# A fused attention and gMLP block on one core: the key load cut in two and the first maxima moved, idle matmuls moved, and h rows computed between the scores and the weighted sum

## The chip, the core and the metric

The kernel runs on one core of a Trainium2 chip. The core has five engines with their own instruction streams: PE (TensorE, matmuls; the profile lists its weight loads apart, as PEld), DVE (VectorE), ACT (ScalarE), POOL (GpSimd) and SP, which here only issues DMAs. Matmul results land in PSUM, of which there are eight banks of 128 x 512 float32; operands lie in SBUF. The metric is the device time of one execution in microseconds (us), the median of several runs.

## What is computed

The reference is a transformer block on 2048 rows of width 512, in float32: attention with 32 heads of width 16, then a gated MLP whose gate mixes the rows.

```python
def _A_ref(x, wqkv, wo):                     # H = 32, Dh = 16
    qkv = ((x @ wqkv).reshape(B, S, 3, H, Dh)).transpose(2, 0, 3, 1, 4)
    scores = jnp.einsum("bhqd,bhkd->bhqk", qkv[0], qkv[1]) * Dh ** -0.5
    o = jnp.einsum("bhqk,bhkd->bhqd", softmax(scores), qkv[2])
    return o.transpose(0, 2, 1, 3).reshape(B, S, D) @ wo
def _B_ref(x, w_in, w_sp, b_sp, w_out):      # S = 2048, D = 512, Fh = 688
    z = gelu(x @ w_in)
    z2 = _layernorm(z[..., Fh:])
    g = jnp.einsum("ts,bsf->btf", w_sp, z2) + b_sp[None, :, None]
    return jnp.einsum("bsf,fd->bsd", z[..., :Fh] * g, w_out)
h = x + _A_ref(_layernorm(x), wqkv, wo)
out = h + _B_ref(_layernorm(h), w_in, w_sp, b_sp, w_out)
```

## The kernel before the change

The program has four stages, one after the other on PE.

**Projections** (up to about 168 us). The rows of x are normalised, transposed and multiplied by wqkv. Each number is held as two rounded parts, so that each product takes three matmuls (`mm3`, lines 92 to 95: the lines L93, L94 and L95 of the profile). One projection of 512 columns is twelve matmuls. `take` (L386 to L390) copies its result out of PSUM: ACT writes the first part (L85), DVE the second (L90), SP stores both to q_scr or k_scr in DRAM (L389). q, k and v come back from there in other layouts: `load_k` (L160) loads the keys of a group of four heads in six DMAs (L164), `load_q` the queries (L193), `load_uv` sums and differences of keys (L172).

**Maxima.** The softmax needs a bound for each row before the scores are used. `max_pair` (L204) returns eight steps per block of rows: each a matmul of queries with keys into one PSUM bank (L222), followed by a DVE maximum over the bank (L227), or by ACT's absolute value (L232) and a DVE combination (L236). In the order of issue, the first six steps touch the key columns 0 to 1535 and the uv tile, the last two the columns 1536 to 2047. The last 24 projections (`for j in range(24)`, L547) are interleaved with the first 88 of these steps: `ahead(6)` issues six of them in the middle of a projection, in the projections that the condition on L555 names. The steps of `ahead` take six PSUM banks in turn, the last four of them four banks in another order (L454).

**Attention** (L708 to L774). A unit is one group of four heads, one block of 512 queries and one block of 128 keys. One pass of the loop handles two units and has this order on PE, with n the number of the first unit (n = 0, 2, ... 510):

```
score, score        # unit n: 2 x 2 matmuls (L663), each followed by an ACT exponential (L666)
step, step          # two maxima steps of a later group
weigh(previous)     # weighted sum of unit n-1: eight matmuls (L674) that read the exponentials
step, step
score, step, score, step   # unit n+1
step
weigh(unit n)
step
```

The maxima run 11 passes ahead, so they end with n = 488, and from n = 490 a third PSUM buffer for scores is opened in the banks that they leave (`ps_l`). In the first pass there is nothing to weigh, and eight matmuls with no use (stand-ins, L735) stand in the place of `weigh(previous)`; they write the bank of the weighted sum, which in the projections was a bank of projection results. After a block of queries `gather` (L677) copies the weighted sum out and SP stores it.

**Rows of h before the end of attention.** `load_o` (L589) loads a block of 128 rows of the attention output and of the reciprocal sums (L593, L596), POOL multiplies them (L600), `split_o` (L603) cuts the product into two parts, `make_h` (L608) multiplies it by wo: twelve matmuls in four `mm3`. Two such blocks are made within the attention loop (L758 to L772): three products after the second weighted sum of each of the eight passes n = 492 to 506. Their splits stand on DVE at n = 490, 498 and 506, the loads behind n = 480, 484, 496 and 504. A block's result is added to x on DVE (L617), its statistics taken (L620, L624, L104 to L120), and it is normalised (L771).

**The MLP** (from about 1414 us) begins with the transpose of the first block (L862), the product of the third block of h (L917), the transpose of the second block, and so on.

The order of the instructions of PE, ACT, DVE and SP is the order of the code, within each of two regions marked `tc.manual_schedule`: one for the projections (L457), one for attention (L710). Where the end of one region and the start of the next fall against each other on an engine, and the whole order of POOL, are left to a scheduler. Each engine works its queue in order; an instruction waits for the data and buffers that it needs.

Of the kernel before, what the change touches and what calls it, by code (L numbers as in the profile page):

```python
# [32 lines left out]
LEAD = 11  # L33
KM = 50
PB = 6
FIRST = 3
RG = 64
VW = DH + 1
FB = [min(i * P, FH - P) for i in range(6)]
# [6 lines left out]
def block_kernel(ctx: ExitStack, tc: tile.TileContext, x, wqkv, wo, w_in, w_sp4, b_sp, w_out, out):  # L46
# [45 lines left out]
    def mm3(ps, lh, ll, rh, rl, first, last):  # L92
        nc.tensor.matmul(ps, lh, rh, start=first, stop=False)  # L93
        nc.tensor.matmul(ps, lh, rl, start=False, stop=False)  # L94
        nc.tensor.matmul(ps, ll, rh, start=False, stop=last)  # L95
# [61 lines left out]
        return 8 * (hg // 2) + 4 * t + 2 * (hg % 2) + p  # L157


    def load_k(hg, pieces=range(6)):  # L160
        for j in pieces:
            j, t = divmod(j, 2)
            h0 = DH * head(hg, 0, t)
            nc.sync.dma_start(  # L164
                kst[hg % 2][RG * t + j:RG * t + KS:3, :, :].bitcast(F32),
                k_scr[(0, 0, 1)[j], h0:h0 + 2 * DH, :].rearrange("(p r) s -> r p s", r=DH))


    def load_uv(hg, pieces=range(3)):
# [95 lines left out]
    with ExitStack() as pre:  # L265
# [180 lines left out]
        def ahead(k):  # L446
            for _ in range(k):
                m = done[0] // 8
                if not todo and m < LEAD:
                    steps = max_pair(m)  # L450
                    todo.extend(steps[i] for i in (0, 1, 3, 2, 4, 6, 5, 7))
                if todo:

                    todo.pop(0)(done[0] % 6 if done[0] < 8 * LEAD - 4 else (3, 0, 1, 2)[done[0] % 4])  # L454
                    done[0] += 1

        with tc.manual_schedule(engines={E.PE, E.Activation, E.DVE, E.SP}):  # L457
            takes = []

            def proj(kind, *which):  # L460

                def between(d):
                    if d == 0 and rest:
                        rest.pop(0)()
                    if d == 1 and takes:
                        takes.pop(0)()

                takes.append(kind(*which, between))

# [24 lines left out]
            put = load_wqk(0)  # L494
            proj(proj_v, 1)
            normal(2, 3)
            turn_x(2, 3)
            for sb in range(8, 12):
                load_x(sb)
            put()  # L500
            for g in range(3):
                a, b = 4 * g, 4 * g + 4
                mv = moments(4)
                if g:
                    proj(proj_v, a)
                    turn_x(a + 2, a + 3)
                    if g == 1:
                        load_x(14)
                        load_x(15)
                    stats(mv, b, b + 1)  # L510
                    proj(proj_v, a + 1)
                    stats(mv, b + 2, b + 3)
                    proj(proj_v, a + 2)
                    normal = scales(mv)
                    normal(b, b + 1)
                    proj(proj_v, a + 3)
                else:
                    proj(proj_v, 2)
                    stats(mv, 4, 5)
                    proj(proj_v, 3)  # L520
                    stats(mv, 6, 7)
                if g == 1:
                    load_q(0)
                proj(proj_qk, 0, g, 1)
                if not g:
                    normal = scales(mv)
                    normal(b, b + 1)
                if g == 2:
                    put = load_wqk(1)
                proj(proj_qk, 0, g, 0)  # L530
                turn_x(b, b + 1)
                if not g:
                    load_x(12)
                    load_x(13)
                normal(b + 2, b + 3)
            proj(proj_v, 12)
            turn_x(14, 15)
            proj(proj_v, 13)
            load_uv(0)
            proj(proj_qk, 0, 3, 1)  # L540
            put()
            proj(proj_qk, 0, 3, 0)
            proj(proj_v, 14)
            load_k(0)
            proj(proj_v, 15)

            for j in range(24):  # L547
                b, n, i = 1 + j // 8, j // 2 % 4, 1 - j % 2

                def between(d):  # L550
                    if d == 0 and takes:
                        takes.pop(0)()
                        if rest:
                            rest.pop(0)()
                    if d == 1 and j >= FIRST and (j % 3 < 2 or j == 23):  # L555
                        ahead(6)
                    if d == 3 and turned:
                        max_rows()

                if j in (2, 10):  # L560
                    put = load_wqk(b + 1)
                if j in (5, 13):
                    put()
                if j == 4:
                    load_v(0)
                if j in (8, 12):
                    load_q(j // 4 - 1)
                if j == 16:
                    fixed(kst[0])
                takes.append(proj_qk(b, n, i, between))  # L570
            takes.pop(0)()
            ahead(8 * LEAD - done[0])
# [27 lines left out]
        nc.gpsimd.tensor_mul(o, o, rc)  # L600
        os_[sb] = o

    def split_o(sb, eh="act"):  # L603
        o = os_.pop(sb)
        o2s[sb] = [e2.tile([P, DB, P], F32R, name=f"o2{i}", bufs=1) for i in range(2)]
        split(o2s[sb][0], o2s[sb][1], o, eh)

    def make_h(sb, acc, steps=range(DB)):  # L608

        o2, h = o2s[sb], xrs[sb]  # L610
        for d in steps:
            mm3(acc, o2[0][:, d, :], o2[1][:, d, :], wo2[0][:, d, :], wo2[1][:, d, :],
                d == 0, d == DB - 1)
        if steps[-1] < DB - 1:
            return
        o2s.pop(sb)
        nc.vector.tensor_add(h, acc, h)  # L617
        nc.sync.dma_start(h_scr[sb * P:(sb + 1) * P, :], h)
        hst[sb] = e2.tile([P, 6], F32, name="st")
        nc.vector.bn_stats(hst[sb], h)  # L620
# [24 lines left out]
    with ExitStack() as at:  # L645
# [47 lines left out]
        def load_weights(i):  # L693
# [11 lines left out]
            nc.sync.dma_start(t, src[:, a, f])  # L705
            split(dst[0][:, a, f], dst[1][:, a, f], t, "pool", "pool")

        units = [(hg, qb, kb) for hg in range(HG) for qb in range(NQ) for kb in range(NB)]  # L708
        prev, turn, later = None, [2], []
        with tc.manual_schedule(engines={E.PE, E.Activation, E.DVE, E.SP}):  # L710
            for n in range(0, len(units), 2):
# [16 lines left out]
                pts = [score(hg, qb, kb, 0), score(hg, qb, kb, 1)]  # L728
                step(2)
                step(0)  # L730
                if prev is None:

                    pv[0] = ps_v.tile([P, 512], F32, name="pv")
                    for j in range(4):
                        nc.tensor.matmul(pv[0][32 * j:32 * j + 32, :], vst[0][:, :32],  # L735
                                         vst[0][:, :512], start=True, stop=True)
                else:
                    weigh(*prev)
                step(1)
                if kb == 0 and n:  # L740
# [3 lines left out]
                step(0)  # L744
                pts1.append(score(hg, qb, kb1, 1))
                step(1)
                step(2)
                weigh(hg, qb, kb, pts)
                if turned:
                    max_rows()  # L750
# [3 lines left out]
                    invert()  # L754
                if n % 32 == 16 and n < 6 * 32:
                    load_weights(n // 32)

                if n in (480, 484, 496, 504):  # L758
                    load_o(h_rows[(480, 484, 496, 504).index(n)])
                if 492 <= n < 508:  # L760
                    i, d = divmod((n - 492) // 2, DB)
                    sb = h_rows[i]
                    if not d:
                        acc = later[0].tile([P, 512], F32, name="h")
                    make_h(sb, acc, [d])
                if n in (490, 498, 506):
                    split_o(h_rows[(n - 490) // 8], None)
                if n in (498, 506):
                    mv, rs = scale_h(sb)
                    hns[sb] = e2.tile([P, D], F32, name="hn", bufs=3)  # L770
                    nc.vector.tensor_scalar(hns[sb], xrs.pop(sb), mv[:, 0:1], rs,  # L771
                                            op0=ALU.subtract, op1=ALU.mult)  # L772
            weigh(*prev)
            gather(*prev[:2], e2)  # L774
    attn.close()
# [496 lines left out]
```

## Time and profile before

| | |
|---|---|
| median of 3 runs | 1874.13 us (1872.52 to 1876.24) |
| the profiled execution | 1873.93 us |
| its span, first to last instruction | 1872.2 us |
| PE busy, share of the span | 99% |
| DVE, ACT, POOL busy | 82%, 70%, 12% |
| attention, first pass to first transpose of the MLP | 168.07 to 1414.34 us |

The profile gives a time and a duration for each instruction, from the start of the span. A row of a timeline has the start, the time, the engine, the line of the code, the operation, the tiles written and read, the number of instructions that were merged into the row, and in brackets how long the engine had been idle before and what released it. A row of the chain of waits has a start, a length and what the program's end hung on in that time. A row of a table by stretches has, after the stretch and its length, the busy time and the number of instructions for PE, PEld, DVE, ACT and POOL, then the granted clock of PE as a share of the full clock, the share of the DMA engines and GB/s. A busy PE can be a PE whose matmul waits, since matmul ends are modelled; so the starts of the matmuls are what to read.

### The profile page before, as it was taken

Reading aid. Unit: us, or ns where it says so; the run is one execution under the profiler, and the core shown is the slowest. Engines: PE = TensorE matmul, PEld = TensorE weight load, DVE = VectorE, ACT = ScalarE, POOL = GpSimd, SP = SyncE. Lnnn points to the kernel's source line nnn. Section 1 sums busy time; section 2 is a strip of 40 time slices with the busy share of each in tenths; the row PEclk is TensorE's granted clock in tenths of the full one; section 3 lists DMA queues with packets and bytes.
Section 4 is the critical chain, followed back from the end, with each engine's and each line's share of the span. In section 5 each row is a group of like instructions: output and inputs, shape, how many; then the busy total and the mean of one; then the engine's idle time right before and its main releaser. Section 6 shows DMA issues by size and latency. Waiting matters only on the chain.

```text
span 1872.2 us, 32341 instructions
## 1 busy us (share of the span) xinstructions
PE 1861.8 (99%) x11606; PEld 1064.2 (57%) x11606; DVE 1527.3 (82%) x3048; ACT 1318.7 (70%) x1696; POOL 222.3 (12%) x300
## 2 busy tenths in 40 slices
PE   9999999999999999999999999999999999999999
PEld 6875444444444444444444444444437999999998
DVE  6478999999999999999999999999936666867654
ACT  3224888888888888888888888888885444434221
POOL 2241000011010100000000000000010756001111
PEclk9999999999999999999999999999999999999999
DMA  6687111221120111022012011100024554768552
GB/s 191 175 223 180 41 24 29 48 54 28 39 56 16 52 40 25 18 47 39 13 38 41 16 38 39 25 13 16 24 58 122 164 161 165 226 189 272 192 190 87
DMA packets 148392, 159.82 MB, mean 85 GB/s; under 512 B 62984, under 2 KB 93208, under 8 KB 146696
## 3 DMA queue, kind: packets, MB, share of 16 engines
q1 hardware_dynamic: 143448, 146.35, 29.0%
q10 hardware_dynamic: 4752, 11.41, 1.6%
q8 instruction: 91, 1.49, 0.3%
q14 instruction: 69, 0.57, 0.1%
q0 software_dynamic: 32, 0.01, 0.0%
HBM read 101.16 MB, written 55.61 MB: 84 GB/s over the span
## 4 chain that ended last, share of the span: by engine, by line
PE 98%; DMA 1%; ACT 0%; SPq 0%; DVE 0%; issue 0%; DVEq 0%; ACTq 0%
PE pv L674 27%; PE m L222 26%; PE s L663 13%; PE acc L93 6%; PE acc L95 6%; PE acc L94 6%; PE g L95 4%; PE g L94 4%; PE g L93 4%; PE tp L1156 1%; DMA kst<-k_scr 1%; PE tp L862 0%; DMA wg<-in_wqkv 0%; PE tp L366 0%; DMA k_scr<-part 0%; PE tp L222 0%
## 5 line engine op out<-in xcount | busy, mean ns | idle before, releaser
L666 ACT ACTIVATE pt<-s 128x1024 f32<-128x1024 f32 x1024 | 994.3, 1030 | 148.9 <-PE s L663 146.1
L227 DVE TENSOR_REDUCE mx<-m 128x1 f32<-128x512 f32 x1508 | 956.2, 683 | 102.2 <-PE m L222 58.7
L222 PE MATMUL m<-kst,qst 48*128 48x512 f32 x1508 | 604.8, 447 | 0.6 <-DMA kst<-k_scr 0.5
L674 PE MATMUL pv<-pt,vst 128*32 128x512 f32 x4096 | 549.6, 605 | 0.3 <-DVE o L682 0.3
L663 PE MATMUL s<-qst,kst 50*128 50x512 f32 x2048 | 465.7, 429 | 0.0
L222 PEld LDWEIGHTS m<-kst,qst 48*128 48x128 f32 x1508 | 262.6, 184 | 317.4 <-DVE mx L227 222.1
L663 PEld LDWEIGHTS s<-qst,kst 50*128 50x128 f32 x2048 | 222.7, 185 | 50.5 <-ACT pt L666 29.4
L222 PE MATMUL m<-uvs,qst 48*128 48x512 f32 x497 | 247.0, 497 | 0.0
L222 PEld LDWEIGHTS m<-uvs,qst 48*128 48x128 f32 x497 | 90.9, 183 | 205.4 <-DVE mx L227 204.6
L674 PEld LDWEIGHTS pv<-pt,vst 128*32 128x32 f32 x4096 | 82.3, 108 | 160.2 <-issue 154.7
L236 DVE CUSTOM_DVE_ANT_0 ab<-m,ab 128x512 f32<-128x512 f32 x249 | 169.1, 679 | 0.0
L232 ACT ACTIVATE ab<-m 128x512 f32<-128x512 f32 x248 | 149.3, 602 | 5.3 <-PE m L222 5.3
L87 POOL CAST mparts<-nm 128x16 fp32r<-128x16 f32 x32 | 6.3, 198 | 877.5 <-DVE nm L242 877.5
L802 ACT ACTIVATE ws<-a 128x512 fp32r<-128x512 f32 x80 | 45.7, 621 | 53.6 <-PE g L95 27.1
L93 PE MATMUL acc<-wi,hT 128*128 128x344 f32 x256 | 83.1, 325 | 0.0
L95 PE MATMUL acc<-wi,hT 128*128 128x344 f32 x256 | 81.7, 319 | 0.0
L94 PE MATMUL acc<-wi,hT 128*128 128x344 f32 x256 | 81.7, 319 | 0.0
L878 ACT ACTIVATE z<-acc 128x344 f32<-128x344 f32 x64 | 29.2, 458 | 63.4 <-PE acc L95 63.2
L803 DVE TENSOR_TENSOR ws<-a,ws 128x512 fp32r<-128x512 f32 x80 | 56.5, 749 | 13.2 <-ACT ws L802 13.1
L93 PE MATMUL g<-b,ws 128*128 128x344 f32 x192 | 62.6, 326 | 0.0
L95 PE MATMUL g<-t,ws 128*128 128x344 f32 x192 | 61.3, 319 | 0.0
L94 PE MATMUL g<-t,ws 128*128 128x344 f32 x192 | 61.2, 319 | 0.0
(202 smaller groups left out, 2147.5 us busy)
## 6 DMA issues: line engine op xcount, KB each, us to landing
a<-in_w_sp SPq DMA_DIRECT2D x80, 256.0 KB
qst<-q_scr SPq DMA_DIRECT2D x192, 64.0 KB
kst<-k_scr SPq DMA_DIRECT2D x48, 256.0 KB
z_scr<-z ACTq DMA_DIRECT2D x32, 344.0 KB
k_scr<-part SPq DMA_DIRECT2D x16, 512.0 KB
q_scr<-part SPq DMA_DIRECT2D x16, 512.0 KB
z<-z_scr SPq DMA_DIRECT2D x14, 344.0 KB
b<-z_scr SPq DMA_DIRECT2D x24, 172.0 KB
```

What stands on the lines that cost most here:

```text
L93: nc.tensor.matmul(ps, lh, rh, start=first, stop=False)
L94: nc.tensor.matmul(ps, lh, rl, start=False, stop=False)
L95: nc.tensor.matmul(ps, ll, rh, start=False, stop=last)
L222: nc.tensor.matmul(acc, q[r, p, c], keys[r, p], start=True, stop=True)
L227: nc.vector.reduce_max(at(t, e if t else e - 1), acc, axis=AX.X)
L232: nc.scalar.activation(ab[0], acc, AF.Abs)
L236: nc.vector.tensor_tensor_reduce(ab[0], acc, ab[0], 0.5, LOW, ALU.add, ALU.max, at(0, 0))
L663: nc.tensor.matmul(s[:, t, :], k[r, p, kb * P:(kb + 1) * P], q[r, p, :], start=True, stop=True)
L666: nc.scalar.activation(t, s, AF.Exp, scale=DH ** -0.5)
L674: nc.tensor.matmul(pv[0][32 * j:32 * j + 32, :], vst[hg % 2][:, c:c + 32], pts[j % 2][:, j // 2, :], start=kb == 0, stop=kb == NB - 1)
L802: nc.scalar.activation(hi, src, AF.Copy)
L803: (nc.gpsimd if el == "pool" else nc.vector).tensor_sub(lo, src, hi.bitcast(F32))
```

## The change

Five things are done.

1. The maxima start two projections sooner: `FIRST` goes from 3 to 1, and the condition becomes `j % 3`, so the calls of `ahead(6)` stand in j = 1, 2, 4, 5, ... 20, and the last four steps in j = 22. The steps use the six banks in turn to the end.
2. The first key load is cut at column 1536. The first part is issued after the projection `proj_v(12)`, the second where the whole load was issued. Six DMAs become twelve.
3. The stand-ins move from the place of `weigh(previous)` to the place behind the fourth score and the sixth maxima step of the first pass.
4. The products of h move ahead of the second weighted sum of a pass, behind the scores: three in the passes n = 490 and 492, two in each of the nine passes 494 to 510. These are the same 24 products. The end of a block (addition, split of the next block, statistics, normalisation) follows its twelfth product.
5. The loads move to n = 476, 482, 492 and 504. The first block is split on POOL behind n = 482, the second on DVE as before, the third on POOL behind the last product of the second, in the pass n = 510.

```diff
-FIRST = 3
+FIRST = 1
-    def load_k(hg, pieces=range(6)):
+    def load_k(hg, pieces=range(6), c=slice(0, S)):
...
-                kst[hg % 2][RG * t + j:RG * t + KS:3, :, :].bitcast(F32),
-                k_scr[(0, 0, 1)[j], h0:h0 + 2 * DH, :].rearrange("(p r) s -> r p s", r=DH))
+                kst[hg % 2][RG * t + j:RG * t + KS:3, :, c].bitcast(F32),
+                k_scr[(0, 0, 1)[j], h0:h0 + 2 * DH, c].rearrange("(p r) s -> r p s", r=DH))
...
-                    todo.pop(0)(done[0] % 6 if done[0] < 8 * LEAD - 4 else (3, 0, 1, 2)[done[0] % 4])
+                    todo.pop(0)(done[0] % 6)
...
             proj(proj_v, 12)
+            load_k(0, c=slice(0, 3 * 512))
             turn_x(14, 15)
...
-            load_k(0)
+            load_k(0, c=slice(3 * 512, S))
...
-                    if d == 1 and j >= FIRST and (j % 3 < 2 or j == 23):
+                    if d == 1 and j >= FIRST and j % 3:
                         ahead(6)
...
+    def h_products(sb, acc):
+        o2 = o2s.pop(sb)
+        for i in range(3 * DB):
+            d, a, b = i // 3, (0, 1, 0)[i % 3], (0, 0, 1)[i % 3]
+            yield nc.tensor.matmul(acc, o2[b][:, d, :], wo2[a][:, d, :], start=i == 0, stop=i == 3 * DB - 1)
...
+        def more_h(k):
+            for _ in range(k):
+                if not pieces:
+                    sb = h_rows[len(hns)]
+                    acc = later[0].tile([P, 512], F32, name="h")
+                    pieces.extend([sb, acc, h_products(sb, acc)])
+                sb, acc, products = pieces
+                next(products)
+                made[0] += 1
+                if made[0] % (3 * DB):
+                    continue
+                pieces.clear()
+                add_h(sb, acc)
+                split_o(h_rows[len(hns) + 1], *("pool", "pool") if hns else [None])
+                mv, rs = scale_h(sb)
+                hns[sb] = e2.tile([P, D], F32, name="hn", bufs=3)
+                nc.vector.tensor_scalar(hns[sb], xrs.pop(sb), mv[:, 0:1], rs,
+                                        op0=ALU.subtract, op1=ALU.mult)
...
-                if prev is None:
-                    pv[0] = ps_v.tile([P, 512], F32, name="pv")
-                    for j in range(4):
-                        nc.tensor.matmul(pv[0][32 * j:32 * j + 32, :], vst[0][:, :32],
-                                         vst[0][:, :512], start=True, stop=True)
-                else:
+                if prev:
                     weigh(*prev)
...
                 pts1.append(score(hg, qb, kb1, 1))
                 step(1)
+                if prev is None:
+                    pv[0] = ps_v.tile([P, 512], F32, name="pv")
+                    for j in range(4):
+                        nc.tensor.matmul(pv[0][32 * j:32 * j + 32, :], vst[0][:, :32],
+                                         vst[0][:, :512], start=True, stop=True)
                 step(2)
+                if n >= 490:
+                    more_h(2 + (n < 494))
                 weigh(hg, qb, kb, pts)
...
-                if n in (480, 484, 496, 504):
-                    load_o(h_rows[(480, 484, 496, 504).index(n)])
-                if 492 <= n < 508:
-                    i, d = divmod((n - 492) // 2, DB)
-                    sb = h_rows[i]
-                    if not d:
-                        acc = later[0].tile([P, 512], F32, name="h")
-                    make_h(sb, acc, [d])
-                if n in (490, 498, 506):
-                    split_o(h_rows[(n - 490) // 8], None)
-                if n in (498, 506):
-                    mv, rs = scale_h(sb)
-                    hns[sb] = e2.tile([P, D], F32, name="hn", bufs=3)
-                    nc.vector.tensor_scalar(hns[sb], xrs.pop(sb), mv[:, 0:1], rs,
-                                            op0=ALU.subtract, op1=ALU.mult)
+                if n in (476, 482, 492, 504):
+                    load_o(h_rows[(476, 482, 492, 504).index(n)])
+                if n == 482:
+                    split_o(h_rows[0], "pool", "pool")
```

`add_h` is the end of `make_h` (L617 to L620) as a function of its own.

More of the change, by code (lines that the diff above doesn't have):

```diff
@@ L601, in load_o, with split_o, make_h, add_h @@
         os_[sb] = o
-    def split_o(sb, eh="act"):
+    def split_o(sb, eh="act", el=None):
         o = os_.pop(sb)
         o2s[sb] = [e2.tile([P, DB, P], F32R, name=f"o2{i}", bufs=1) for i in range(2)]
[L606 to L616, printed above, removed]
+        split(o2s[sb][0], o2s[sb][1], o, eh, el)
+    def h_products(sb, acc):
[3 more added lines that the diff above has]
+            yield nc.tensor.matmul(acc, o2[b][:, d, :], wo2[a][:, d, :], start=i == 0, stop=i == 3 * DB - 1)
+    def make_h(sb, acc):
+        for _ in h_products(sb, acc):
+            pass
+        add_h(sb, acc)
+    def add_h(sb, acc):
+        h = xrs[sb]
         nc.vector.tensor_add(h, acc, h)
@@ L706, in load_weights @@
             split(dst[0][:, a, f], dst[1][:, a, f], t, "pool", "pool")
+        pieces = []
+        def more_h(k):
[10 more added lines that the diff above has]
+                pieces.clear()
+                add_h(sb, acc)
+                split_o(h_rows[len(hns) + 1], *("pool", "pool") if hns else [None])
[3 more added lines that the diff above has]
+                                        op0=ALU.subtract, op1=ALU.mult)
+        made = [0]
         units = [(hg, qb, kb) for hg in range(HG) for qb in range(NQ) for kb in range(NB)]
```

## The prediction

> **What bounds the kernel.** I read the page's busy times first, then the table by stretches, then the chain of waits where PE's order changes.
>
> ```profile
> PE 1861.8 (99%) x11606; PEld 1064.2 (57%) x11606; DVE 1527.3 (82%) x3048; ACT 1318.7 (70%) x1696; POOL 222.3 (12%) x300
> ...
> 400.00:1300.00 900.00, 900.00 (x5912) 371.18 (x5908) 827.41 (x1570) 795.30 (x947) 30.46 (x81) 1.00 0.15 32
> ```
>
> PE is the bound: between 400 and 1300 us it is busy without a break at the full clock, while DVE is busy 92% and ACT 88%. The change adds no matmul and removes none, and the passes between the first and n = 490 keep their order. So it can only win where PE waits or other engines hold it up. Three such places lie at the edited lines.
>
> First, the load of the keys (SP and PE rows of the timeline, then the chain of waits):
>
> ```profile
> 70.75 0.37 SPq L389 DMA_DIRECT2D q_scr<-part  x1
> 74.00 0.33 SPq L429 DMA_DIRECT2D v_scr<-v  x1
> 82.73 3.74 SPq L164 DMA_DIRECT2D kst<-k_scr  x6
> 95.46 0.74 PE L222 MATMUL m<-kst,qst 48*128 48x512 f32 x3 [0.47 <-DMA kst<-k_scr]
> ...
> 78.70 4.02 DMA k_scr<-part
> 85.88 9.44 DMA kst<-k_scr
> ```
>
> The first maxima step stands still 0.47 us for the last of six key DMAs, which landed at 85.88 + 9.44 = 95.32.
>
> Second, the seam from projections to attention (chain of waits, stretches, ACT's rows):
>
> ```profile
> 168.14 0.47 PE s L663 x2
> 168.73 0.88 issue
> 169.61 0.60 ACT part L85
> 170.23 0.70 DVE part L90
> 171.07 1.07 PE pv L735 x8
> ...
> 174.45 1.59 PE pv L674 x8
> 176.04 0.43 PE m L222
> ...
> 180.91 0.43 PE m L222
> ...
> 169.50:170.00 0.50, 0.00 (x0) 0.00 (x0) 0.50 (x1) 0.50 (x2) 0.00 (x0) 1.00 0.83 291
> ...
> 172.50:173.00 0.50, 0.50 (x6) 0.36 (x3) 0.19 (x1) 0.22 (x1) 0.00 (x0) 0.50 1.14 328
> ...
> 175.50:176.00 0.50, 0.50 (x6) 0.03 (x2) 0.29 (x2) 0.00 (x0) 0.00 (x0) 0.87 0.77 176
> ...
> 168.69 1.02 ACT L666 ACTIVATE pt<-s 128x1024 f32<-128x1024 f32 x1 [3.46 <-PE s L663]
> 170.08 1.03 ACT L666 ACTIVATE pt<-s 128x1024 f32<-128x1024 f32 x1
> ...
> 169.45 0.69 DVE L227 TENSOR_REDUCE mx<-m 128x1 f32<-128x512 f32 x1 [0.59 <-PE m L222]
> ```
>
> The stand-ins wait until 171.07 for the copy of the last projection (L85, L90), since they write its bank, and everything behind them on PE waits too. The clock then falls to 0.50 until about 175.6. The first pass lasts 176.04 - 168.14 = 7.90 us, the next 4.87: 3.03 us lie in the seam, the most that can be won there.
>
> Third, the tail from n = 490 (chain of waits: its first row, one pass with products of h, the end; then the waits of that stretch):
>
> ```profile
> 1365.50 0.43 PE m L222
> ...
> 1396.37 0.67 PE s L663 x4
> 1397.04 0.99 PE pv L674 x8
> 1398.03 0.67 PE s L663 x4
> 1398.70 1.25 PE pv L674 x8
> 1399.95 0.43 PE h L93
> 1400.38 0.23 PE h L94
> 1400.61 0.23 PE h L95
> ...
> 1411.41 3.00 PE pv L674 x16
> 1414.40 0.59 PE tp L862 x4
> ...
> ACT pt L666 <- PE s L663: 6.3, 9, 0.8
> ...
> 1396.90 3.77 ACT L666 ACTIVATE pt<-s 128x1024 f32<-128x1024 f32 x4 [0.70 <-PE s L663]
> ```
>
> A pass is 4.47 us: scores 0.67, sum 0.99, scores 0.67, sum 1.25, products 0.89. The second sum takes 0.26 more than the first, because it waits for exponentials. Then the products hold back the next scores, and ACT idles 0.70. PE and ACT wait for each other in turn.
>
> **Key load: -0.47.** The first block of steps was due at 95.46 - 0.47 = 94.99. Two projections are 24 products at 0.23 (the row "PE h L94" has that spacing), 5.5 us, so it is now due at 89.5, and needs columns 0 to 1535. SP is free for their six DMAs at 70.75 + 0.37 = 71.1. They cannot take longer than the whole load, 95.32 - 82.73 = 12.6, so they land by 83.7: hidden. On SP they go ahead of the store of v (74.00, now 74.9), the uv load and the store of the last k block (78.70, now about 79.3). That store lands 4.02 later, at 83.3, and the second part issues until 83.3 + 3.74 = 87.0. It is needed by the second block, twelve products later, at 92.3 or after. A quarter of the bytes in a quarter of the last transfer's 9.44 is 2.4, so it lands by 89.4. If the last small DMA, issued at about 86.4, took the full 9.44, PE would wait 3.5. I take the quarter, the nearer in bytes, and keep 3.5 as the bad end. The steps themselves and their switches move, in the same number.
>
> **Seam: -1.2** (bounds 0.5 slower, below, and 3.03 faster). I count from the first score. Now the six banks are free: the last four steps were issued one and a half projections (4 us) before, and DVE needs 4 x 0.69 for them. The first three maxima go at 0.6 to 0.8. The copy of the last projection stays where the scheduler put it, between the two exponentials: these end at 1.64 (168.69 + 1.02 - 168.07) and 3.04, and the second projection copy on DVE at 2.86. The first DVE maximum ends at 1.8, the second, behind that copy, at 3.5. So the fourth maximum goes at 1.8, the third score at about 2.0, the fifth maximum at 3.5, the fourth score beside it. The sixth needs the absolute values, which ACT makes behind the second exponential: 3.0 + 0.6 (as L85's 0.60) = 3.6. Then stand-ins from about 4.1 to 5.2, the seventh maximum 0.43, the sum 0.99 at full clock: 6.7 against 7.90. What is late next is the second DVE maximum, with PE idle about 1 us instead of 1.66 in one piece. If the scheduler puts the copy ahead of both exponentials, all this comes some 0.7 earlier. I take 1.2.
>
> The Trainium skill, "TensorE: Matmul & The Clock Gate", section "Why this matters for your kernels", says that gaps up to some 3 us do not cost the clock. This case's trace does not agree: 1.66 us without a matmul stood ahead of 3.5 us at 0.50. By the page the first rival would have no chance, and the sum stays.
>
> **Tail: -3.5.** With two products between the scores and the second sum a pass is 0.67 + 0.99 + 0.67 + (0.43 + 0.23) + 0.99 = 3.98 us, with three 4.21. The second sum starts 2.99 after the first score; the exponentials that it reads end at about 0.55 + 2 x 0.94 = 2.4 (3.77 for four), so it waits no more. ACT needs 3.77 and stays just under PE's 3.98. Eleven passes are 2 x 4.21 + 9 x 3.98 = 44.2; with the last sum, 0.99, and 0.2 for the maxima step at the start 45.4, against 1414.40 - 1365.50 = 48.90. No row shows a sum right behind full-array products; I take the 0.99 that it has behind scores. The best end is ACT without its waits, -6.3 from the row of nine; the bad end is the second rival.
>
> **Edits at nothing.** The split of the first block, now on POOL, stands behind the multiplication of the second block:
>
> ```profile
> 1349.67 0.58 SPq L593 DMA_DIRECT2D o<-o_scr  x1
> 1357.87 1.29 POOL L600 TENSOR_TENSOR o<-o,rc 128x512 f32<-128x512 f32 x1 [29.32 <-DMA rc<-r_scr]
> ...
> 67.77 0.62 POOL L87 CAST wqk<-wg 128x512 fp32r<-128x512 f32 x1
> 68.47 1.30 POOL L90 TENSOR_TENSOR wqk<-wg,wqk 128x512 fp32r<-128x512 f32 x1
> ...
> 1405.36 0.69 DVE L617 TENSOR_TENSOR xr<-h,xr 128x512 f32<-128x512 f32 x1 [12.86 <-PE h L95]
> 1409.70 0.55 DVE L771 TENSOR_SCALAR hn<-xr,mv,rs_r 128x512 f32<-128x512 f32 x1
> ```
>
> The second load takes the SP slot behind the stores of n = 480, at 1349.67; its multiplication ends at 1357.87 + 1.29 = 1359.2, the split at 1361.1. The first product comes at about 1368.0 (1365.50 + 0.43 + the first scores, sum and second scores, with its waits): 6.9 us of cover. Behind its twelfth product the first block's DVE work (addition, statistics, the split's cast and its subtraction, none above the addition's 0.69: at most 2.8) has 3.3 (two sums, two pairs of scores) until the next product. At the end of the tail two sums and a transpose (1.0 + 1.0 + 0.6, with the switch) lie between the last product and the third block: POOL's 0.62 is ready, and its 1.30 ends about 2.4 behind, 0.8 ahead of its use. The second block's DVE chain lasted 1409.70 + 0.55 - 1405.36 = 4.9 with a split in it, 3.8 without; its transpose comes 2.6 + 12 x 0.23 = 5.4 behind the last product. It delays the copy of the last weighted sum by 1.7, which nothing near reads.
>
> The Trainium skill, "SBUF — State Buffer", section "SBUF: two separate sides", says that POOL and some DVE operations hold their shared port in turn. By it the split of the third block could hold up that chain by up to its length, an estimate of 0.5 us for PE; no row here shows such a pair.
>
> **Sum.** The profiled execution took 1873.93, 1.73 more than its span and 0.20 under the median of 1874.13. 1873.93 - 0.47 - 1.2 - 3.5 = 1868.8.
>
> **Rivals.** *The clock falls again at the seam.* For it: an idle of 1 us in pieces is not far from the 1.66 that did it. Against it: no piece is as long. The next pass is bound by PE, and 3.5 us at half clock cost it 1.75: the seam then loses 0.5 instead of winning 1.2, giving 1870.5.
>
> *The products cost more between scores and sum than behind it* (the change doesn't do what it says: a new switch eats the recovered waits). A switch shows as 0.43 instead of 0.23 at the first product; 0.2 to 0.43 more in each of eleven passes is 2.2 to 4.7, so 1871.0 to 1873.5; I put it at 1872. Against it: behind scores the sum already has a switch in its 0.99.
>
> *POOL's split comes late.* In POOL's queue it stands behind a multiplication that waits for DMAs; the row above waited 29.32, and 8.2 passed from the load's first issue. Past the cover of 6.9 each us is one of PE. It decides the sign from 1873.93 + 3.75: it must be 8.9 later than the cover, 16 us later than before. At that point the time is 1877.7, and with a further 1.3 for one more multiplication ahead of it 1879. Against it: the same load landed in time in the same SP slot.
>
> **Chances.** 0.2% is 3.75 us, about what a measurement of this kernel can tell from no change. The forecast has 0.68; its own range goes from 1865.0 (most of both bounds at seam and tail) to 1870.2 (half of seam and tail lost). Clock 0.14, switch 0.13: both within 0.2%. Late split 0.05, slower. So faster 0.68, same 0.27, slower 0.05. The range 1865.0 to 1872.4 takes in the clock and half of the switch, and the key load's 3.5; it leaves out about 0.15.
>
> **What would show it.** Right: no wait of L222 for kst; the clock at 1.00 in all stretches from 165 to 185, and under 7 us from the first score to the second pass; about 4.0 us from one first sum to the next from n = 494, with the second sum at 0.99, and ACT's idle at 0.2 to 0.3; the first transpose about 5 us sooner. Wrong: a first L222 waiting at 89 or 93; a stretch at 0.50; a second sum above 1.2 in the tail, or a product of h behind POOL.

## The result and the profile after

The changed kernel takes **1869.04 us** (median of 11 executions, 1868.64 to 1872.01) against 1874.13 (11 executions, 1872.44 to 1877.11) of the kernel before: a ratio of 0.9973 with an interval of 0.9964 to 0.9982. The profiled execution took 1870.97 us, its span 1869.2. It is one of the two in eleven in which the mean granted clock was below 1.000; the nine others took 1868.64 to 1869.47. That matters below, since two profiles are only compared well at the same clock.

The page's busy times of the changed kernel; as before PE is nearly all of the span:

```profile
PE 1859.8 (99%) x11606; PEld 1062.2 (57%) x11606; DVE 1525.2 (82%) x3044; ACT 1319.1 (71%) x1696; POOL 225.1 (12%) x304
```

PE's busy time fell by 2.0 and the span by 3.0. The changed execution was already 0.77 late before the first edited instruction (its store of q at 71.52 against 70.75), which hides some of the gain from the difference of the spans; so each place is read by itself. The lateness came back in the repeated runs below, where the same store stands at 71.58 and 70.79.

**The keys.** SP's rows of the timeline: the first part has gone at 75.8, the second stands between two stores.

```profile
71.52 0.37 SPq L389 DMA_DIRECT2D q_scr<-part  x1
71.97 3.83 SPq L164 DMA_DIRECT2D kst<-k_scr  x6
...
80.47 0.38 SPq L389 DMA_DIRECT2D k_scr<-part  x1
82.33 0.37 SPq L389 DMA_DIRECT2D q_scr<-part  x1
87.37 3.74 SPq L164 DMA_DIRECT2D kst<-k_scr  x6
```

Its queue's own waits between 80 and 95 us (in all, times, longest):

```profile
SPq L164 <- DMA k_scr<-part: 4.6, 1, 4.6
```

The chain of waits of the same kernel, first two blocks of maxima steps:

```profile
90.08 0.23 PE acc L95
90.30 0.66 PE m L222 x3
...
93.90 0.23 PE acc L95
94.13 0.66 PE m L222 x3
```

Both blocks follow the last product of their half projection at the usual spacing. No step waits for a key.

**The seam.** The chain of waits from the end of the last projection to the second pass:

```profile
168.20 0.03 ACTq L85
...
168.28 0.61 ACT part L85
...
168.91 0.69 DVE part L90
169.60 0.61 DVE mx L227
...
170.25 0.50 PE m L222
...
171.81 1.35 PE pv L775 x8
...
173.88 1.86 PE pv L681 x8
175.75 0.43 PE m L222
```

The table by stretches of it (after the times: PE, PEld, DVE, ACT, POOL, then the clock):

```profile
172.00:172.50 0.50, 0.50 (x8) 0.00 (x0) 0.50 (x2) 0.50 (x2) 0.00 (x0) 0.81 0.90 168
172.50:173.00 0.50, 0.50 (x4) 0.00 (x0) 0.18 (x1) 0.50 (x1) 0.00 (x0) 0.50 0.44 90
...
175.50:176.00 0.50, 0.50 (x6) 0.31 (x4) 0.00 (x0) 0.00 (x0) 0.00 (x0) 0.77 1.03 119
```

And two rows of its timeline:

```profile
168.77 1.94 ACT L673 ACTIVATE pt<-s 128x1024 f32<-128x1024 f32 x2
170.25 0.50 PE L222 MATMUL m<-kst,qst 48*128 48x512 f32 x1 [0.93 <-DVE mx L227]
```

The first pass lasts 175.75 - 168.20 = 7.55 us against 7.90. The scheduler put the copy of the last projection ahead of both exponentials on ACT and ahead of the first maximum on DVE; the fourth maxima step waits 0.93 for that maximum. The clock fell here too, from about 172.3 to 175.7.

**The tail.** The chain of waits: its start, one pass with products, its end.

```profile
1365.74 0.43 PE m L222
...
1376.72 0.66 PE h L614 x2
1377.38 0.99 PE pv L681 x8
1378.38 0.67 PE s L670 x4
1379.05 0.99 PE pv L681 x8
1380.04 0.66 PE s L670 x4
1380.70 0.66 PE h L614 x2
...
1409.23 2.43 PE pv L681 x16
1411.66 0.59 PE tp L882 x4
...
1415.03 0.44 PE tp L882 x4
```

The waits between 1360 and 1415 us (in all, times, longest):

```profile
ACT pt L673 <- PE s L670: 3.8, 12, 0.6
```

A pass is 1380.70 - 1376.72 = 3.98 us, and every sum behind products takes 0.99. From the first row to the first transpose are 1411.66 - 1365.74 = 45.92 us against 48.90: 2.98 less. The last two sums take 2.43 together, not 1.99: the last one waits 0.45 for its exponentials.

### The profile page after: what moved, and what is told of

The parts are those of the page before. It is cut to its first block, busy times and chain, and to the rows that moved or that the text cites. A ratio compares the mean times of both kernels' runs of the same rounds, so it can differ in the third digit from the quotient of the medians.

```text
span 1869.2 us, 32350 instructions
## 1 busy us (share of the span) xinstructions
PE 1859.8 (99%) x11606; PEld 1062.2 (57%) x11606; DVE 1525.2 (82%) x3044; ACT 1319.1 (71%) x1696; POOL 225.1 (12%) x304
## 4 chain that ended last, share of the span: by engine, by line
PE 99%; DVE 1%; ACT 0%; DMA 0%; issue 0%; SPq 0%; DVEq 0%; ACTq 0%
PE pv L681 27%; PE m L222 26%; PE s L670 13%; PE acc L93 6%; PE acc L95 6%; PE acc L94 6%; PE g L95 4%; PE g L94 4%; PE g L93 4%; PE acc L614 2%; PE tp L1176 1%; PE h L614 0%; PE tp L882 0%; PE tp L366 0%; ACT xT L85 0%; PE tp L222 0%
## 5 line engine op out<-in xcount | busy, mean ns | idle before, releaser
L85 ACT ACTIVATE part<-acc 128x512 fp32r<-128x512 f32 x32 | 19.1, 597 | 60.9 <-PE acc L95 56.4
L95 PE MATMUL g<-t,ws 128*128 128x344 f32 x192 | 61.3, 319 | 0.0
## 6 DMA issues: line engine op xcount, KB each, us to landing
b<-z_scr SPq DMA_DIRECT2D x24, 172.0 KB
```

## The experiments

Theory: the gain is the tail's order (about 3 us) and the seam's (about 1), the key load at most 0.5, and the POOL splits cost nothing. Rivals: the clock at the seam decides, or the stand-ins' move does. Times are medians; "at 1.000" are the executions whose mean granted clock was 1.000, and the last column is against the kernel before at 1.000 on the same chip, which took 1873.12 for the first four rows, 1872.54 for the next four and 1872.87 for the last two. Executions of one kernel at 1.000 scatter by 0.6 to 2.5 us, so a difference of some 0.5 in that column decides nothing.

| kernel | median, us | ratio to before (interval) | at 1.000 | against before at 1.000 |
|---|---|---|---|---|
| changed, again | 1869.64 | 0.9982 (0.9973 to 0.9991) | 1869.22, 7 of 11 | -3.9 |
| before, again | 1873.83 | 1.0003 (0.9994 to 1.0012) | 1873.12, 6 of 11 | 0 |
| tail alone | 1870.21 | 0.9980 (0.9971 to 0.9989) | 1870.14, 8 of 11 | -3.0 |
| head alone | 1872.24 | 0.9994 (0.9985 to 1.0003) | 1872.18, 9 of 11 | -0.9 |
| no stand-ins | 1867.62 | 0.9966 (0.9955 to 0.9977) | 1867.45, 5 of 7 | -5.1 |
| stand-ins in the old place | 1868.27 | 0.9973 (0.9961 to 0.9984) | 1868.21, 5 of 6 | -4.3 |
| key load whole | 1878.98 | 1.0028 (1.0017 to 1.0039) | none of 7 | |
| three products in each pass | 1869.75 | 0.9977 (0.9968 to 0.9986) | 1869.46, 8 of 11 | -3.1 |
| splits on DVE | 1869.88 | 0.9979 (0.9970 to 0.9988) | 1869.57, 8 of 11 | -3.3 |
| two stand-ins, old place | 1867.55 | 0.9966 (0.9954 to 0.9979) | 1867.55, 5 of 5 | -5.3 |

### Both kernels again

No edit. The kernels were run once more to see the seam in other executions.

> The changed kernel once more, for the clock of each run. In the first set its runs fell into two groups: nine between 1868.64 and 1869.47 us with a mean clock of 1.000, and two at 1870.97 (the profiled one) and 1872.01 with 0.999 and 0.998. Theory (the clock at the seam decides): runs with clock 1.000 near 1869.0, runs with 0.999 about 2 us longer, and if the profile is taken in a run with 1.000, no stretch between 165 and 185 us below 1.00, and the first pass at about 6.5 us instead of 7.6. Rival (the two groups have another cause, such as the time of the first DMAs): a profile at 1.000 still shows the stretch at 0.50.

> The kernel before once more, for the clock of each run, which the first set gives for the changed kernel alone. Theory (the clock at the seam falls in every run of before, and in two of eleven of the changed kernel): all runs at 0.999 or lower, medians near 1874. Rival (the clock falls as seldom here, and the gain has nothing to do with it): most runs at 1.000.

Both profiles came at clock 1.000. The chain of waits of the changed kernel:

```profile
168.29 0.03 ACTq L85
...
171.90 1.00 PE pv L775 x8
...
173.33 0.99 PE pv L681 x8
174.33 0.43 PE m L222
```

And of the kernel before:

```profile
167.54 0.47 PE s L663 x2
...
174.27 0.42 PE m L222
```

The table by stretches of the kernel before, at the place where the clock had fallen in its first profile:

```profile
172.00:173.00 1.00, 1.00 (x7) 0.50 (x3) 0.97 (x2) 1.00 (x2) 0.00 (x0) 1.00 0.98 231
```

And one row of each timeline, the changed kernel's first:

```profile
170.34 0.50 PE L222 MATMUL m<-kst,qst 48*128 48x512 f32 x1 [0.93 <-DVE mx L227]
...
170.46 1.06 PE L735 MATMUL pv<-vst 128*32 128x512 f32 x8 [1.65 <-DVE part L90]
```

At the full clock the first pass is 6.73 us before and 6.05 after (by the starts in the timelines; the rows of the chain, rounded, give 6.04): the order wins **0.68**. The half clock cost 7.90 - 6.73 = 1.17 in the first pass before, and 7.55 - 6.05 = 1.50 after. PE's idle time ahead of the fall is the same in the executions with and without it (1.66 and 1.65 us before, 0.93 both times after), so an idle time of that length does not make the clock fall each time. The first maxima step before came at 94.94 here, straight behind its products: the wait for the key is not in each execution either. The tail alone, which has the old key load too, had none in its profile (its first step follows a product of 95.22 at 95.53).

### The two halves of the change

Tail alone: everything of the head is put back (`FIRST = 3` with its condition and bank order, one key load, the stand-ins ahead of the third step).

```diff
-FIRST = 1
+FIRST = 3
...
-            load_k(0, c=slice(0, 3 * 512))
...
-            load_k(0, c=slice(3 * 512, S))
+            load_k(0)
```

> Only the tail is changed: products of h ahead of the second sum, loads and splits as in the changed kernel; first maxima, key load and stand-ins as before. Theory (the tail is worth what its passes show, 48.90 against 45.92 us): 3.0 us under the kernel before, passes of 3.98 us from n = 494. Rival (the tail gives little, and the seam's clock is the gain): within 1 us of before. The clock at the seam should fall as in before.

Head alone: products, splits and loads of h as before.

```diff
-                if n >= 490:
-                    more_h(2 + (n < 494))
...
+                    for _ in range(3):
+                        next(made[0])
```

> Only the head is changed: first maxima two projections sooner, key load in two parts, stand-ins behind the first maxima; the tail as before, passes of 4.47 us. Theory (key load 0.5 and the seam 1.5, mostly the clock, which stays up in most runs): 2.0 us under the kernel before, in two groups 2 us apart by the clock. Rival (the head was worth only its 0.5 and the 0.3 that the two profiles show at the seam): 0.8 us under before.

At 1.000 the tail wins 3.0 and the head 0.9, together 3.9, and both in one kernel 3.9: the parts add up. Tail alone has passes of 3.98 and the old first pass of 6.73; head alone has a first pass of 6.03. For the head's 0.9 the seam gives 0.7; what is left is of the size of the scatter and of the key's 0.47.

### The stand-ins

No stand-ins at all (they compute nothing that is used):

```diff
-                if prev is None:
-                    pv[0] = ps_v.tile([P, 512], F32, name="pv")
-                    for j in range(4):
-                        nc.tensor.matmul(pv[0][32 * j:32 * j + 32, :], vst[0][:, :32],
-                                         vst[0][:, :512], start=True, stop=True)
```

> The changed kernel without the stand-ins of the first pass (eight matmuls whose result nothing uses). In executions with a mean clock of 1.000 the changed kernel takes 1869.1 us. Theory (behind the sixth maximum PE is the bound, so the stand-ins cost their 1.0 us): first pass 5.05 instead of 6.05 us, 1868.1. Rival (they fill a wait, for the seventh maximum's bank or for the clock): no change at 1.000, and the clock falls in more than half of the executions, which puts the median 1 us above the changed kernel's.

The four stand-ins in their old place, with all else of the change kept:

```diff
-                if prev:
+                if prev is None:
+                    ...
+                else:
                     weigh(*prev)
```

> The changed kernel with the stand-ins in their old place, behind the first two maxima; the maxima stay two projections sooner, so that the six banks are free. Theory (there they wait for the last projection's copy, until 1.4 us behind the first score, and hold up the third maximum, hence ACT's absolute values and the sixth maximum): first pass 6.5 to 6.7 us against 6.05, 0.5 us slower at a clock of 1.000. Rival (in that place they fill PE's wait of 0.93 us for DVE, and the order costs nothing): 6.1 us, the same time, and fewer falls of the clock.

Without stand-ins the kernel is 1.2 us faster at 1.000 (-5.1 against the changed kernel's -3.9). Its first pass lasted 5.04 us in the profile, 0.2 of that from a clock that fell in its last half microsecond, against 6.05. The profiled execution was the one of the seven with the lowest clock (1871.65 us), and its table by stretches shows what that means:

```profile
172.00:172.50 0.50, 0.50 (x4) 0.00 (x0) 0.50 (x2) 0.38 (x1) 0.00 (x0) 0.51 0.12 41
...
182.00:182.50 0.50, 0.50 (x3) 0.04 (x1) 0.29 (x2) 0.48 (x1) 0.00 (x0) 0.75 0.52 66
```

One fall lasted from 172.0 to 182.25. So the stand-ins cost some 1.0 to 1.2 in the place of the change, as my theory had it. The rival's long fall exists as well: this one execution of seven lost about 4 us by it.

Back in the old place they cost far less, and there **my theory fell**: it had that place slower by 0.5. The timeline and the chain of that kernel, which ran at 1.000:

```profile
168.94 1.07 PE L765 MATMUL pv<-vst 128*32 128x512 f32 x8 [0.56 <-DVE part L90]
```

```profile
167.50 0.03 ACTq L85
...
171.75 0.99 PE pv L681 x8
172.75 0.43 PE m L222
```

The first pass lasts 5.25 instead of 6.05. With the maxima sooner, the copy that the stand-ins wait for is done at 168.9, and PE would stand still until about 169.5 in any case, for DVE's first maximum. There they lie beside a wait; in the new place they lie behind it, alone on PE. By the first passes the move itself loses 0.8 us that the earlier maxima had won; the column at 1.000 shows 0.4 of it (-4.3 against -3.9), a difference within the scatter.

Two stand-ins in that old place:

```diff
-                    for j in range(4):
+                    for j in range(2):
```

> The changed kernel with its stand-ins in their old place, ahead of the third maxima step, and two of them instead of four. Theory (stand-ins in the old place lie inside PE's wait for DVE of 0.93 us, where four last 1.07 behind a wait of 0.56 for the copy): two last about 0.55, end ahead of the maximum that the next step waits for, so at clock 1.000 the first pass is 5.05 to 5.27 us and the time 1867.9 to 1868.2, 0 to 0.3 under the four. Rival (the fewer stand-ins, the oftener and the longer the clock falls, as without them, where one fall lasted 10 us): more than 3 of 10 executions below 1.000, those at 1869 to 1872, and a median over the 1868.27 of the four.

The timeline's row:

```profile
168.88 1.05 PE L765 MATMUL pv<-vst 128*32 128x512 f32 x4 [0.56 <-DVE part L90]
```

Two calls (four matmuls in the trace) take 1.05 where four calls (eight matmuls) take 1.07, so the theory's 0.55 was wrong, and the first pass is the same 5.24. Nothing speaks for the rival: all five executions ran at 1.000. This kernel has the lowest median, 1867.55 (1867.51 to 1868.11), 1.5 under the changed kernel's 1869.04. Between the two profiled executions at 1.000 (1867.51 and 1869.56) the first pass accounts for 0.8, and another 0.8 lies ahead of every edited line: the store of q stands at 70.76 here and at 71.58 there. Why the start differs is not known, so it is no gain of the stand-ins; and the intervals of the ratios overlap.

### The key load

Maxima sooner, but the key loaded whole where it was:

```diff
-            load_k(0, c=slice(0, 3 * 512))
...
-            load_k(0, c=slice(3 * 512, S))
+            load_k(0)
```

> The changed kernel with the first keys loaded whole, where the kernel before loads them. Theory (the first maxima are due at 90.3 us and the keys land at 95.3): PE waits 5.0 us at L222, and the clock falls behind it, 3.5 us at half, so 5 to 6.7 us slower than the changed kernel, 1874.1 to 1875.8. Rival (the steps that need early columns go ahead, or the time lost is won back at the seam, where DVE is ahead): under 2 us slower.

It was 1878.98: worse than the theory and the rival said. The timeline and the table by stretches:

```profile
94.33 0.73 PE L222 MATMUL m<-kst,qst 48*128 48x512 f32 x3 [4.39 <-DMA v_scr<-v]
```

```profile
96.00:98.00 2.00, 2.00 (x6) 1.52 (x6) 1.93 (x5) 0.00 (x0) 0.00 (x0) 0.50 0.86 233
...
178.00:180.00 2.00, 2.00 (x10) 0.34 (x9) 0.69 (x1) 0.91 (x1) 0.00 (x0) 0.50 0.53 104
```

The step stands still 4.39 us. (The transfer that the row names is a store issued behind the key load; the step reads kst.) The clock is at 0.50 for 3.4 us behind it, and in the seam for 6.8: about 1.7 and 3.4 us more of PE's time. 4.4 + 1.7 + 3.4 = 9.5, against the 9.3 between this profiled execution (1878.55) and the changed kernel at 1.000 (1869.22, on another chip). The theory had the wait and the stretch behind it, and missed the two at the seam. One execution of the seven (1874.87, mean clock 0.999) came out as the theory had it; the six others had 0.995 to 0.997. The earlier maxima need the cut load; without it they lose more than the whole change wins.

### The order of the tail

Three products in each of eight passes, none in the last three:

```diff
-                if n >= 490:
-                    more_h(2 + (n < 494))
+                if 490 <= n < 506:
+                    more_h(3)
```

> The changed kernel with three products of h in each of the passes n = 490 to 504, ahead of the second sum, and none in 506 to 510. Theory (PE's work sets a pass with products, 4.21 us with three and 3.98 with two, and ACT's four exponentials, 3.77 us with their pitch, set one without, where PE has only 3.32): 8 x 4.21 + 3 x 3.77 = 45.0 against 2 x 4.21 + 9 x 3.98 = 44.2, so 0.8 us slower. Rival (PE's total work is the bound whatever its spread): the same time.

The chain of its last passes:

```profile
1403.59 1.17 PE pv L681 x8
...
1407.26 3.00 PE pv L681 x16
1410.26 0.59 PE tp L882 x4
```

The tail is 46.66 us long, 0.74 more than the changed kernel's, as the theory had it. The passes without products are bound by ACT: from their second sum on, a sum takes 1.17 to 1.27 instead of 0.99, because it waits for its exponentials, and the last two take 3.00, as before the change. Two products a pass keep PE's 3.98 just above ACT's 3.77 to the end.

Splits back on DVE:

```diff
-                split_o(h_rows[len(hns) + 1], *("pool", "pool") if hns else [None])
+                split_o(h_rows[len(hns) + 1], None)
...
-                    split_o(h_rows[0], "pool", "pool")
+                    split_o(h_rows[0], None)
```

> The changed kernel with all three splits of the tail's blocks back on DVE (and ACT for the cast, as before). Theory (prediction): in the changed kernel the splits on POOL cost nothing, and the place of a split matters only through DVE's chain ahead of the second transpose, 3.8 us without and 4.9 with a split, against 5.4 of cover: so 0 to +0.5 us, 1869.0 to 1869.6 for executions at clock 1.000 (the changed kernel 1869.1). Rival (the splits had to leave DVE and ACT, since ACT has only 0.2 us of slack in a pass): ACT's cast of 0.3 to 0.6 us per block and DVE's subtraction delay exponentials and maxima, +0.5 to +2 us, 1869.6 to 1871.1.

A row of the timeline at the end of its tail:

```profile
1414.15 0.66 PE L882 MATMUL tp<-ident,hn 128*128 128x128 f32 x4 [0.24 <-DVE hn L734]
```

The tail is the same 45.92 to the first transpose. The second transpose waits 0.24 and takes 0.66 instead of 0.44: 0.45 in all, the upper end of the theory. So the splits on POOL win about half a microsecond, at one place. The casts of these splits ran on DVE (L89, 0.41 each), here as before the change, and not on ACT as the expectation has it; so the rival's load on ACT was not put to the test.

## Why the prediction was right, step by step

**What bounds the kernel: right.** All of the change lies where PE waits or is held up; the tail alone and the head alone add up to it.

**Key load, -0.47: right in the profile, small in truth.** No step waits for a key any more. The second part was issued at 87.37, not 83.3, because it waited 4.6 for the store of the k block ahead of it to land; it still landed in time. But the repeated run of the kernel before had no wait to remove, and nor had the tail alone.

**Seam, -1.2: mechanism right, size wrong.** At the full clock it is 0.68. The term set a first pass at half clock (7.90) against one worked out at the full clock (6.7), and so counted a fall of the clock as gained. The working also kept the copy of the last projection between the exponentials; the scheduler put it ahead of both, the case that the text called 0.7 earlier. It came to a first pass of 6.05, 0.65 under the 6.7. What the prediction did not see is that the stand-ins would have fitted into the wait that is left: 0.8 us were to be had by leaving them.

**Clock rival: it happened in the profiled execution.** The first pass there is 7.55. The executions of the changed kernel with a mean clock of 0.999 took about 1870.8, those at 1.000 about 1869.1: a fall costs 1.7, where the rival had 1.75. But it differs between executions of one kernel: 16 of the changed kernel's 22 executions had a mean clock of 1.000. The kernel before had its mean clock below 1.000 in 46 of 79. By the prediction's own list of signs, a stretch at 0.50 and a first pass not under 7 us were to show it wrong; the first profiled execution has both, the repeated one has neither.

The Trainium skill, "TensorE: Matmul & The Clock Gate", section "Why this matters for your kernels", names idle gaps above some 3 us between matmuls as what drops the clock. These runs don't agree: 0.93 us and 1.66 us were each followed by a stretch at 0.50 in one profiled execution, and by none in another. The 4.39 us of the whole key, above that length, were followed by one, and none of that kernel's seven executions kept a mean clock of 1.000.

**Tail, -3.5: mechanism right, 0.5 too much.** The pass came out as worked out, 3.98, and the sum behind products takes the assumed 0.99. Missing is the last sum: in all other passes scores stand ahead of it (0.66), at the end nothing does, and it waits 0.45 for its exponentials. 45.4 + 0.45 is 45.85 against 45.92. The switch rival is refuted by the same 3.98.

**Edits at nothing: right.** No product waits for POOL's split, so the late split did not come. The working had the first split behind the second multiplication, ending at 1361.1; the scheduler put it ahead of that multiplication, and it ended at 1348.3 (POOL's rows of the first profile of the changed kernel). DVE's chain was not the 3.8 of the prediction but 5.1 (from the addition at 1407.76 to the end of the normalisation at 1412.89 in the repeated run of the changed kernel), because the copy of the transposed first block stands in it. It still fits, and with a split in it, as in the last experiment, it doesn't.

The Trainium skill, "SBUF — State Buffer", section "SBUF: two separate sides", would have POOL's split hold up DVE's chain through the shared port, if its instructions are of the kind that takes that port. The chain's addition and statistics took 0.69 each beside POOL's split, and 0.69 each without it (splits on DVE); these two show no hold-up. Whether other pairs of instructions are held up is not shown.

**The sum.** 1868.8 was forecast and 1869.04 measured, but not by its own terms. At clock 1.000 the change wins 3.9 to 4.0, not 5.17: seam and tail were 0.5 too large each, and the key's 0.47 is not in every execution. In the two repeated profiles, both at 1.000, the spans differ by 3.2 (1871.0 and 1867.8), and the changed one is 0.8 late at the store of q, so it wins 4.0 behind it: 0.68 at the seam and 3.04 in the tail (48.96 against 45.92), with 0.3 spread over the rest. The first transpose came 2.7 us sooner in the first pair of profiles and 3.15 in the second, where the list of signs had about 5. The other 1.1 of the 5.09 between the medians is that the kernel before had a fall of the clock in most of its executions and the changed one in few. Whether the change causes that isn't settled: the tail alone, with the seam left as it was, also ran at 1.000 in 8 of 11, and where the falls of unprofiled executions lie was not seen. Part of the agreement is luck. One sum of the prediction is wrong without an effect on its range: with half of seam and tail lost, 1.2 and 3.5, the time is 1871.1, not 1870.2.

## What to carry to other kernels

Filler work belongs inside the wait that it fills: find the wait by its row, and move the filler with it when the wait moves. Before a pass is priced by another pass, look at the granted clock of both; a duration at half clock is no saving of an order. Where two engines take turns, put the spare work of the longer one between the product and its reader, evenly over the passes, so that its pass stays just longer than the other's to the last.

## What the hardware showed that I had not expected

The stretches at half clock have whole lengths. With the share of the half clock in the first and the last stretch they last 3.41 us (172.22 to 175.63) in the kernel before, 3.42 in the changed one, 3.41 and 6.83 with the whole key, and 10.24 without stand-ins: one, one, one, two and three times 3.41. The Trainium skill, "TensorE: Matmul & The Clock Gate", section "Part 1: The HAM clock gate (the "warmup" mystery)", says that PE's activity is judged over a window of 3413 ns that runs on its own, whatever the kernel does; the lengths agree. The starts agree too: with the whole key the two falls, at 95.24 and 177.16, are 81.92 apart, 24 times 3.413. So in one execution all changes of the clock lie on one grid.

That the same 0.93 us cost a stretch in one execution and none in another could then come from idle time that lies in one window here and is shared by two there. The traces speak against it. At the end of each profiled execution, where PE has no work, the clock falls once more, also where it had not fallen at the seam, and from there the grid can be counted back. Two rows by stretches, of the changed kernel's repeated run and of the kernel before's:

```profile
1867.00:1867.50 0.50, 0.00 (x0) 0.00 (x0) 0.00 (x0) 0.00 (x0) 0.00 (x0) 0.96 0.00 0
...
1872.00:1872.50 0.50, 0.00 (x0) 0.00 (x0) 0.00 (x0) 0.00 (x0) 0.00 (x0) 0.60 0.00 0
```

They put these last falls at 1867.46 and 1872.10; in the first profiles they are at 1868.74 (changed) and 1872.06 (before), and the last is 498 windows of 3.4133 us behind that execution's fall at 172.22. Counted back, the windows at the seam are:

| kernel, execution | window | idle time of PE | clock behind it |
|---|---|---|---|
| before, first | 168.80 to 172.22 | 169.41 to 171.07 | 0.50 |
| before, repeated | 168.85 to 172.26 | 168.81 to 170.46 | 1.00 |
| changed, first | 168.90 to 172.31 | 169.32 to 170.25 | 0.50 |
| changed, repeated | 167.62 to 171.04 | 169.41 to 170.34 | 1.00 |

In all four the idle time lies in one window, but for 0.04 us in one of them, and in two of the four the clock did not fall. So neither its length nor a window's edge through it decides alone. What else the window held differs: in the changed kernel the eight stand-ins start in the window ahead of the fall, and none of them in the other. But with three products in each pass (last fall at 1868.23) the window 168.39 to 171.81 holds the whole 0.93 and the eight stand-ins too, and no fall followed. What decides stays open. Why there were two and three stretches in two cases was not found either; PE had work all through them.

Two and four calls of matmuls that each fill 32 of the 128 columns, on a group of 32 columns each, take the same time, 1.05 and 1.07 us, as if each group worked for itself.
